# Attention chunks 6 to 11 in halves of 64 tokens on 64x64 tiles, within a fused attention, FFN and expert kernel

## The chip, the cores and the metric

The kernel runs on one core of a Trainium2 chip. The metric is the device time of one execution in microseconds (us); lower is better. Engines are named as the profile names them: PE is TensorE (PEld its weight loads), DVE is VectorE, ACT is ScalarE, POOL is GpSimd, SP is SyncE, which issues most transfers.

## What is computed

Three layers follow each other on 1536 tokens (2 sequences of 768) with a model width of 512. First comes linear attention with decay, 8 heads of width 64, in blocks of 64 tokens:

```python
for b in range(nb):                       # nb = 768 / 64
    qb, kb, vb = (q[:, :, sl], k[:, :, sl], v[:, :, sl])
    intra = einsum('bhic,bhjc->bhij', qb, kb) * Dmask[None]
    intra = einsum('bhij,bhjd->bhid', intra, vb)
    inter = einsum('bhid,bhde->bhie', qb * lam_pow[None], kv_state)
    out[:, :, sl] = intra + inter
    kv_state = lam_block * kv_state + einsum('bhsd,bhse->bhde', kb * rev_pow, vb)
```

`Dmask` holds the powers of each head's decay `lam` below the diagonal. The second layer is a feed-forward block, `elu(x @ w_in) @ w_out`, with an inner width of 2048. The third sends each token that passes a gate to one of 8 experts (inner width 1024) and adds the weighted result. All of it is float32.

## The kernel before

**Chunks.** The kernel takes tokens in 12 chunks of 128, six to a sequence (`CPS`), three to an FFN block of 384 tokens (`CPB`). A chunk holds two of the reference's blocks, which is the same computation with a mask of 128x128 per head and a state that is carried every 128 tokens. Per chunk there are four groups of fp32 matmuls on TensorE. `at_scores` (L246) multiplies keys by queries, 8 matmuls on 64 of the 128 rows of the array each, two heads side by side. `at_pv` (L295) multiplies values by masked scores, 8 matmuls on 64 columns of the array each. `at_inter` (L310) multiplies the state by decayed queries, 4 matmuls on the whole array; the state of two heads stands as a block-diagonal 128x128 matrix. `at_kv` (L338) multiplies decayed keys by values, 8 matmuls on 64 columns each with 64 moving columns. An fp32 matmul shows as two instructions, each with its weight load. Chunks 0 and 6 begin a sequence and lack the product with the state; chunks 5 and 11 end one and have no keys by values.

**Around them.** VectorE applies the mask (`at_mask`, L256) and adds to the state (`at_state`, L363, L365). GpSimd scales queries (`at_qd`, L273), keys (`at_kdec`, L279) and, from chunk 6 on, the old state (`at_decay`, L350). The result leaves PSUM as a rounded part by ScalarE (`at_evac_hi`, L318) and a rest by VectorE (`at_evac_lo`, L324); the FFN multiplies both parts in three passes.

**The FFN.** `ff1_mm` (L390) is 12 matmuls of 384 columns into a bank of tag h, of which there are two. ScalarE takes relu and exp from it (`ff1_act`, L395, L398), VectorE the max (`ff1_max`, L410), ScalarE rounds (`ff1_hi`, L416), and VectorE takes the rest (`ff1_lo`, L421). `ff2` (L437) is three matmuls of 512 columns for one chunk of tokens.

**Order.** From L641 on, every engine runs in the order in which the program is written. The first part follows the list `PLAN`, which holds chunks 0 to 5, the conversion of the FFN weights on ScalarE and VectorE, and the first FFN steps. Then come steps numbered n, from J = 24 on. In a step the program writes: max and rounding of step n + 1, `ff1_mm(n + 2)`, what the lists Y and A hold for n, `ff1_lo(n + 1)`, `ff2(n, 0)`, `ff2(n, 1)`, `ff1_act(n + 2)`, list B, `ff2(n, 2)`, list Z. Chunks 6 to 8 have their scores at steps 24, 26 and 28 (`at_S`, list A) and everything else at 25, 27 and 29 (`at_P`); chunks 9 to 11 have them at 37, 39, 41 and at 38, 40, 42. `at_P` ends with the load of chunk c + 2 on SyncE's queue (L227, L230). The routing of a finished chunk to its expert (`route_T` transposes, `route_pick` takes logits and the largest, `route_rank`, `route_slot` and `route_send` place it) for chunks 0 to 2 starts at steps 25, 26 and 27, one part a step.

**Banks.** PSUM has eight banks: two of tag h, three of tag y and three of tag aux. `aux()` takes from y in steps 24 to 31 and from aux otherwise. A new tile waits until the last reader of the bank that it is given is done.

Of the kernel before, what the change touches and what calls it, by code (L numbers as in the profile page):

```python
# [8 lines left out]
F32 = mybir.dt.float32  # L9
# [7 lines left out]
P = 128  # L17
# [7 lines left out]
NTOK = NBLK * TB  # L25
NCH = NTOK // P
CPS = 6
LEAD = 21
TAIL1 = 8
E = 8  # L30
# [29 lines left out]
def kernel(  # L60
# [35 lines left out]
    def aux():  # L96
        return bank(aux_tag[0], 3)
# [134 lines left out]
    def load_chunk(c, eng=None):  # L232
        alloc_chunk(c)
        dma_kq(c, eng)
        dma_kv(c, eng)
# [46 lines left out]

    o_t = {}

    def at_pv(c, b=None):
        first = c not in o_t
        if first:
            o_t[c] = b if b is not None else aux()
        o = o_t[c]
        v = kv_t[c]  # L290
        for hp in range(4):
            cs = slice(hp * P, (hp + 1) * P)
            for j in range(2):
                h = 2 * hp + j
                nc.tensor.matmul(  # L295
                    out=o[64 * j:64 * j + 64, cs], lhsT=v[:, 1, h * D:(h + 1) * D],
                    rhs=pm_t[c, j][:, hp, :], start=(first and hp == 0),
                    stop=(not first or c % CPS == 0),
                    skip_group_check=True,
                )  # L300
        del pm_t[c, 0], pm_t[c, 1]

    def at_inter(c, b=None):
        if c % CPS:
            qd = qd_t.pop(c)
            first = c not in o_t
            if first:
                o_t[c] = b if b is not None else aux()
            for hp in range(4):
                nc.tensor.matmul(out=o_t[c][:, hp * P:(hp + 1) * P], lhsT=state[:, hp, :],  # L310
                                 rhs=qd[:, hp, :], start=(first and hp == 0), stop=not first,
                                 skip_group_check=True)

    def at_evac_hi(c):
        b, cc = divmod(c, CPB)
        if b not in xT:
            xT[b] = mid.tile([P, 2, 4, TB], F32R, tag="xT", name="xT", bufs=2)
        nc.scalar.activation(out=xT[b][:, 0, :, cc * P:(cc + 1) * P],  # L318
                             in_=o_t[c].rearrange("p (k i) -> p k i", k=4), func=ACTF.Copy)

    def at_evac_lo(c):
        b, cc = divmod(c, CPB)
        ts = slice(cc * P, (cc + 1) * P)
        nc.vector.tensor_tensor(out=xT[b][:, 1, :, ts],  # L324
                                in0=o_t.pop(c).rearrange("p (k i) -> p k i", k=4),
                                in1=xT[b][:, 0, :, ts].bitcast(F32), op=ALU.subtract)

    s_t = {}

    def at_kv(c):  # L330
        if c % CPS == CPS - 1:
# [254 lines left out]
    if True:  # L586
# [127 lines left out]
        for item in PLAN.split():  # L714
            op, args = item.split(":")
            run[op](*map(int, args.split(",")))
            if item == "F1:1":
                tables()
        nc.sync.dma_start(out=wg, in_=wgs.rearrange("(k p) e -> p k e", p=P))
        init_slots()  # L720
        for n in range(LEAD, J):
# [18 lines left out]
        A, B, C, Y, Z = {}, {}, {}, {}, {}  # L740
        early = None

        def at_S(c):
            at_scores(c)
            at_qd(c)
            for half in range(2):
                at_mask(c, half)
            at_kdec(c)

        def at_P(c):  # L750
            at_pv(c)
            at_inter(c)
            at_decay(c)
            at_kv(c)
            at_evac_hi(c)
            at_state(c)
            at_evac_lo(c)
            if c + 2 < NCH:
                load_chunk(c + 2)

        def put(d, n, f, *a):
            d.setdefault(n, []).append((f, a))
# [7 lines left out]
                put(Y, n + 2 + i, route_slot, c0 + i)  # L770
                put(B, n + 2 + i, route_send, c0 + i)

        for i in range(CPB):
            put(A, J + 2 * i + 1, at_P, CPS + i)
            put(A, 2 * NF + 6 + 2 * i, at_P, CPS + CPB + i)
        put_routes(J + 1, 0)
        put_routes(2 * NF, CPB)
        for i in range(CPB):
            put(A, J + 2 * i, at_S, CPS + i)
            put(A, 2 * NF + 5 + 2 * i, at_S, CPS + CPB + i)  # L780
        put_routes(3 * NF, 2 * CPB)
        for n in range(3 * NF, N):
            f = n - 3 * NF
# [324 lines left out]
def layout(inputs):  # L1108
    import numpy as np

    def pair(a):
        a = _chunks(a).reshape(2, 4, 2, CPS, P, D)
        return a.transpose(0, 3, 2, 5, 1, 4).reshape(NCH, P, 4, P)

    def rows(a):
        return _chunks(a)[:, :, :, ::-1].transpose(0, 2, 3, 1, 4).reshape(NCH, P, DM)

    q, k, v = inputs["q"], inputs["k"], inputs["v"]
    def words(a):
        return a.view(np.int64) if a.dtype == np.float64 else a  # L1120

    w_in = words(np.ascontiguousarray(inputs["moe_w_in"])).reshape(4, P, NF, P).transpose(2, 1, 0, 3).reshape(NF, P, DM)
# [12 lines left out]
```

## Time and profile before

| | us |
|---|---|
| median of 3 runs (lowest, highest) | 460.17 (458.51, 460.31) |
| the profiled execution | 458.31 |
| its span, first to last instruction | 456.6 |
| PE busy | 442.7 (97%) |
| DVE busy | 294.1 (64%) |
| ACT busy | 240.3 (53%) |
| POOL busy | 78.4 (17%) |

The profile is of one execution. A busy time is the time in which at least one instruction of the engine is in progress, so matmuls that overlap count once. The granted TensorE clock was 0.997 of full speed over the span.

### The profile page before, as it was taken

How to read it: one execution, taken by the hardware profiler on the slowest of the kernel's cores; microseconds unless marked ns; L12 is line 12 of the kernel's file. 1: busy time of each engine (PE TensorE's matmuls, PEld its weight loads, DVE VectorE, ACT ScalarE, POOL GpSimd, SP SyncE). 2: the span in 40 equal slices, each digit the busy share in tenths (PEclk: the TensorE clock that was granted, in tenths of full speed). 3: DMA queues.
4: the chain of work that ended last, by engine and by line, in shares of the span. 5: the costliest groups of instructions: out<-in, count | busy, mean ns of one | idle time of the engine just before them, and what ended most of it. 6: DMA issues, size and time to landing. Idle time of an engine off the chain costs nothing.

```text
span 456.6 us, 7006 instructions
## 1 busy us (share of the span) xinstructions
PE 442.7 (97%) x2679; PEld 385.9 (85%) x2679; DVE 294.1 (64%) x557; ACT 240.3 (53%) x398; POOL 78.4 (17%) x100
## 2 busy tenths in 40 slices
PE   8899999999999999999999999999999999999993
PEld 7778889878998888998888889889988788888872
DVE  4899999999333455345333324665536688999970
ACT  3465776667344322433222444565653788888840
POOL 4532002200100224104321000130003102222201
PEclk9999999999999999999999999999999999999998
DMA  8999602896001221300020006335248789999401
GB/s 309 407 418 419 246 0 92 248 120 189 0 2 69 94 95 61 134 0 34 16 77 1 0 1 253 105 127 198 93 139 319 260 295 391 363 365 375 175 17 33
DMA packets 26106, 74.65 MB, mean 164 GB/s; under 512 B 4018, under 2 KB 9146, under 8 KB 24016
## 3 DMA queue, kind: packets, MB, share of 16 engines
q1 hardware_dynamic: 24032, 68.99, 42.7%
q0 software_dynamic: 1600, 3.03, 1.8%
q10 hardware_dynamic: 432, 2.10, 1.2%
q8 instruction: 23, 0.38, 0.3%
q14 instruction: 19, 0.16, 0.1%
HBM read 65.82 MB, written 10.51 MB: 167 GB/s over the span
## 4 chain that ended last, share of the span: by engine, by line
PE 76%; DVE 9%; issue 5%; ACT 3%; POOL 2%; DMA 2%; SPq 1%; POOLq 0%; DVEq 0%; ACTq 0%
PE h L390 24%; PE y L437 19%; PE h L918 8%; PE y L943 6%; PE aux L437 5%; DVE v L172 2%; DVE v L175 2%; DMA xe<-blank 2%; PE aux L310 1%; PE aux L295 1%; PE aux L492 1%; PE aux L246 1%; PE aux L929 1%; ACT v L157 1%; PE y L246 1%
## 5 line engine op out<-in xcount | busy, mean ns | idle before, releaser
L390 PE MATMUL h<-xT,wa 128*128 128x384 f32 x480 | 90.1, 338 | 0.0
L390 PEld LDWEIGHTS h<-xT,wa 128*128 128x128 f32 x480 | 83.8, 188 | 3.1 <-DVE e L410 0.4
L437 PE MATMUL y<-wa,g 128*128 128x512 f32 x270 | 70.8, 401 | 0.9 <-DVE g L421 0.9
L395 ACT ACTIVATE e<-h 128x384 f32<-128x384 f32 x64 | 31.1, 486 | 53.2 <-PE h L390 53.1
L437 PEld LDWEIGHTS y<-wa,g 128*128 128x128 f32 x270 | 48.9, 188 | 11.6 <-DVE g L421 1.8
L416 ACT ACTIVATE g<-e 128x384 fp32r<-128x384 f32 x64 | 33.4, 522 | 43.3 <-DVE e L410 43.1
L410 DVE SCALAR_TENSOR_TENSOR e<-e,h 128x384 f32<-128x384 f32 x64 | 35.1, 548 | 31.5 <-ACT e L398 31.5
L390 PE MATMUL h<-xT,wb 128*128 128x384 f32 x288 | 54.3, 338 | 0.0
L390 PEld LDWEIGHTS h<-xT,wb 128*128 128x128 f32 x288 | 50.5, 188 | 1.8
L421 DVE TENSOR_TENSOR g<-e,g 128x384 fp32r<-128x384 f32 x64 | 37.8, 591 | 16.0 <-ACT g L416 15.9
L437 PE MATMUL y<-wb,g 128*128 128x512 f32 x162 | 40.5, 395 | 0.0
L918 PE MATMUL h<-wa,xgT 128*128 128x512 f32 x144 | 36.1, 397 | 0.1
L569 POOL DMA_INDIRECT xe<-x,idx x12 | 12.1, 1009 | 139.7 <-DVE s L542 58.0
L437 PEld LDWEIGHTS y<-wb,g 128*128 128x128 f32 x162 | 30.0, 188 | 5.7 <-DVE g L421 0.2
L398 ACT ACTIVATE e<-e 128x384 f32<-128x384 f32 x64 | 33.6, 525 | 2.0
L918 PEld LDWEIGHTS h<-wa,xgT 128*128 128x128 f32 x144 | 26.5, 188 | 5.7 <-ACT xgT L468 0.3
L135 DVE TENSOR_TENSOR wa<-big,wa 128x1024 fp32r<-128x1024 f32 x22 | 26.6, 1234 | 4.3 <-ACT wa L134 4.1
L943 PE MATMUL y<-wa,ht 128*128 128x512 f32 x96 | 23.7, 398 | 0.0
L135 DVE TENSOR_TENSOR wa<-ahead,wa 128x1024 fp32r<-128x1024 f32 x18 | 21.6, 1246 | 2.9 <-ACT wa L134 2.7
L134 ACT ACTIVATE wa<-big 128x1024 fp32r<-128x1024 f32 x22 | 22.4, 1058 | 1.2 <-DMA big<-in_wex_dram 1.2
L437 PE MATMUL aux<-wa,g 128*128 128x512 f32 x90 | 23.0, 397 | 0.0
L952 POOL TENSOR_TENSOR o<-o,xg 128x512 f32<-128x512 f32 x7 | 9.1, 1294 | 71.5 <-ACT o L951 62.2
(205 smaller groups left out, 682.4 us busy)
## 6 DMA issues: line engine op xcount, KB each, us to landing
big<-in_wex_dram SPq DMA_DIRECT2D x17, 1024.0 KB, 5.0
ahead<-in_wex_dram SPq DMA_DIRECT2D x15, 1024.0 KB, 7.0
wb<-in_wff_dram SPq DMA_DIRECT2D x10, 1024.0 KB, 14.5
big<-in_wff_dram SPq DMA_DIRECT2D x5, 1024.0 KB, 17.5
big<-in_kq_dram SPq DMA_DIRECT2D x6, 512.0 KB, 3.5
big<-in_kv_dram SPq DMA_DIRECT2D x6, 512.0 KB, 4.3
out_dram<-x SPq DMA_DIRECT2D x12, 256.0 KB, 2.2
xg<-xe SPq DMA_DIRECT2D x8, 257.0 KB, 7.2
```

Of the source, the lines that this page charges most:

```text
L134: nc.scalar.activation(out=w[:, 0, cs], in_=src, func=ACTF.Copy)
L135: nc.vector.tensor_tensor(out=w[:, 1, cs], in0=src, in1=w[:, 0, cs].bitcast(F32), op=ALU.subtract)
L390: nc.tensor.matmul(out=h, lhsT=w[:, wi, k * P:(k + 1) * P], rhs=xT[b][:, xi, k, :], start=(j == 0), stop=(j == 11))
L395: nc.scalar.activation(out=e, in_=h_t[n], func=ACTF.Relu, scale=-1.0)
L398: nc.scalar.activation(out=e_t[n], in_=e_t[n], func=ACTF.Exp, scale=-1.0)
L410: nc.vector.scalar_tensor_tensor(out=e, in0=e, scalar=-1.0, in1=h_t.pop(n), op0=ALU.add, op1=ALU.max)
L416: nc.scalar.activation(out=g[:, 0, :], in_=e, func=ACTF.Copy)
L421: nc.vector.tensor_tensor(out=g[:, 1, :], in0=e_t.pop(n), in1=g[:, 0, :].bitcast(F32), op=ALU.subtract)
L437: nc.tensor.matmul(out=y_t[b, t], lhsT=g[:, gi, t * P:(t + 1) * P], rhs=w[:, wi, 512:1024], start=(f == 0 and i == 0), stop=(f == NF - 1 a ...
L569: sc = nc.gpsimd.indirect_dma_start(out=xe[:, :], out_offset=bass.IndirectOffsetOnAxis(ap=idx[:, c:c + 1], axis=0), in_=x2[:, :], in_offse ...
L918: nc.tensor.matmul(out=h, lhsT=xgT_t[e][:, xi, k * P:(k + 1) * P], rhs=w_t[NF + 8 * e + k][:, wi, j * 512:(j + 1) * 512], start=(i == 0), ...
L943: nc.tensor.matmul(out=y, lhsT=ht[:, hi, k, :], rhs=w_t[NF + 8 * e + 4 + k // 2][:, wi, (k % 2) * 512:(k % 2) * 512 + 512], start=(i == 0) ...
```

## The change

In chunks 6 to 11 the halves of 64 tokens are treated as blocks of their own, as the reference has them: the mask is 64x64 per head, the state moves every 64 tokens, and every matmul runs on one of the four 64x64 tiles of the array. All of it that falls in a step is put into one function, `at_X(c, nxt)`: products by values and state of chunk c, then keys by values and scores of the following chunk, then a drain of TensorE and the rest of chunk c's state products. `at_X2` evacuates, loads, and updates the state. There are four such steps for three chunks (24, 26, 28, 29 and 37, 39, 41, 42). The state is a ring of three 64-column tables in `state` and `lp`, updated by four operations on VectorE for each half; queries are scaled into a spare half of `mask`; keys are scaled a step earlier. The excursion's second bank is one of tag h. In chunks 0 to 5 the products stay on 128 tokens, and the state product becomes eight matmuls of 64 columns of the array. The head order in the rows of x changes, and `w_in` is reordered before launch to match. The routing of chunks 0 to 2 moves to steps 25, 27 and 30, with `route_pick` in the step of its `route_T`.

```diff
+    def put_o(c, s, b, kb, lhsT, rhs, n=SB):
+        banks, begun = o_t[c]
+        o = banks[s][SB * b:SB * b + SB, kb * n:(kb + 1) * n]
+        nc.tensor.matmul(out=o, lhsT=lhsT, rhs=rhs, start=(s, b) not in begun, stop=True,
+                         skip_group_check=True)
+        begun.add((s, b))
...
     def at_inter(c, b=None):
         if c % CPS:
             qd = qd_t.pop(c)
-            for hp in range(4):
-                nc.tensor.matmul(out=o_t[c][:, hp * P:(hp + 1) * P], lhsT=state[:, hp, :],
-                                 rhs=qd[:, hp, :], start=(first and hp == 0), stop=not first,
-                                 skip_group_check=True)
+            o_bank(c, b)
+            for kb in range(4):
+                for b in range(2):
+                    hp, a = 2 * (kb // 2) + b, kb % 2
+                    put_o(c, 0, b, kb, state[:, hp, SB * a:SB * a + SB], qd[:, hp, :], P)
...
+    def at_tables():
+        nc.gpsimd.tensor_copy(out=mask[0:SB, :, 0:SB], in_=mask[0:SB, :, SB:P])
+
+    def at_scores2(c, banks):
+        t = kq_t[c]
+        for k in range(4):
+            for a, m in ((0, 0), (1, 1), (0, 1), (1, 0)):
+                r, ts = slice(SB * a, SB * a + SB), slice(SB * m, SB * m + SB)
+                nc.tensor.matmul(out=banks[a][ts, k * SB:(k + 1) * SB], lhsT=t[r, 0, k, ts],
+                                 rhs=t[r, 1, k, SB * (1 - m):SB * (2 - m)],
+                                 start=True, stop=True, skip_group_check=True)
...
+    def at_kv2(c, banks, off=0):
+        t = kv_t[c]
+        for k in range(4):
+            for a, m in ((0, 1), (1, 1)) if last_of(c) else ((0, 1), (1, 0), (1, 1), (0, 0)):
...
+    def at_state2(c, s):
+        if last_of(c) and s:
+            return
+        src, prev = s_t[c][1 - s], state_of(c, s)
+        st_t[2 * c + s + 1] = st = ring3[(2 * c + s) % 3]
+        if prev is None:
+            nc.vector.tensor_copy(out=st, in_=src)
+        else:
+            for k in range(4):
+                nc.vector.scalar_tensor_tensor(out=st[:, k, :], in0=prev[:, k, :],
+                                               scalar=lp[:, k, SB - 1:SB], in1=src[:, k, :],
+                                               op0=ALU.mult, op1=ALU.add)
...
+    def at_out(c, banks):
+        t, pm = kv_t[c], pm_t.pop(c)
+        o_t[c] = banks, set()
+        for kb in range(4):
+            for b, r in ((0, 0), (1, 1), (1, 0), (0, 1)):
+                h, rows = 4 * (kb // 2) + 2 * b + kb % 2, slice(SB * r, SB * r + SB)
+                put_o(c, 1 - r, b, kb, t[rows, 1, h * D:(h + 1) * D], pm[rows, h % 2, h // 2, :])
+        for m in range(2):
+            for b, r in ((0, 0), (1, 1), (1, 0), (0, 1)):
+                inter(c, r, m, 1 - r, b)
+
+    def at_out2(c):
+        nc.tensor.drain()
+        for m in range(2):
+            for b, r in ((0, 0), (1, 1), (1, 0), (0, 1)):
+                inter(c, r, m, r, b)
...
+        def at_X(c, nxt):
+            if c is not None:
+                at_out(c, [aux(), aux()])
+            if nxt is not None:
+                banks = [aux(), bank("h", 2)]
+                at_kv2(nxt, banks, 4 * SB)
+                at_scores2(nxt, banks)
+            if c is not None:
+                at_out2(c)
+            if nxt is not None:
+                for a in range(2):
+                    at_mask2(nxt, a)
+
+        def at_X2(c, nxt):
+            if c is not None:
+                at_evac_hi(c)
+                at_evac_lo(c)
+                if c + 2 < NCH:
+                    load_chunk(c + 2)
+            if nxt is not None:
+                at_state2(nxt, 0)
+                at_qd2(nxt)
...
+        def put_chunks(n, c0):
+            for c, nxt, m in ((None, c0, n), (c0, c0 + 1, n + 2), (c0 + 1, c0 + 2, n + 4),
+                              (c0 + 2, None, n + 5)):
+                put(A, m, at_X, c, nxt)
+                put(B, m, at_X2, c, nxt)
+                if nxt is not None:
+                    if m > J:
+                        put(B, m - 1, at_kdec2, nxt)
+                    put(Z, m, at_state2, nxt, 1)
+
+        at_kdec2(CPS)
+        put_chunks(J, CPS)
+        put_chunks(2 * NF + 5, CPS + CPB)
+        for n, c in zip((J + 1, J + 3, J + 6), range(CPB)):
+            put(B, n, route_T, c)
+            put(Z, n, route_pick, c)
+            put(Z, n, route_exp, c)
+            put(Y, n + 1, route_rank, c)
+            put(Y, n + 1, route_slot, c)
+            put(B, n + 1, route_send, c)
```

## Rows read from the trace of the kernel before

**Rows 1.** The page's busy times: us, share of the span, instructions.
```profile
PE 442.7 (97%) x2679; PEld 385.9 (85%) x2679; DVE 294.1 (64%) x557; ACT 240.3 (53%) x398; POOL 78.4 (17%) x100
```
**Rows 2.** Windows, chunks 9 to 11: length, then each engine's busy us (PE, PEld, DVE, ACT, POOL).
```profile
215.92:252.89 36.97, 36.97 (x280) 31.77 (x278) 13.11 (x25) 10.50 (x21) 9.21 (x12) 1.00 0.10 32
```
**Rows 3.** Chain of waits, chunk 5: start us, us, what.
```profile
33.66 1.93 POOL qd L273
...
37.06 1.13 PE aux L310 x8
...
54.75 1.15 DVE v L172
```
**Rows 4.** TensorE's timeline, steps 37 on: start us, us, engine, line, operation.
```profile
215.92 2.25 PE L390 MATMUL h<-xT,wa 128*128 128x384 f32 x12
218.10 1.16 PE L246 MATMUL aux<-big 64*128 64x128 f32 x16
...
221.40 2.26 PE L390 MATMUL h<-xT,wa 128*128 128x384 f32 x12
223.59 1.09 PE L295 MATMUL aux<-t,big 128*64 128x128 f32 x16
224.61 1.16 PE L310 MATMUL aux<-t,state 128*128 128x128 f32 x8
225.70 0.69 PE L338 MATMUL aux<-big 128*64 128x64 f32 x16
226.32 2.36 PE L437 MATMUL y<-wa,g 128*128 128x512 f32 x9
228.52 2.25 PE L390 MATMUL h<-xT,wa 128*128 128x384 f32 x12
...
252.89 2.25 PE L390 MATMUL h<-xT,wb 128*128 128x384 f32 x12
...
257.06 2.25 PE L390 MATMUL h<-xT,wb 128*128 128x384 f32 x12
```
**Rows 5.** TensorE's timeline, chunks 1 and 2, two groups of one tiling.
```profile
20.75 1.05 PE L295 MATMUL y<-pm_store,wb 128*64 128x128 f32 x16
21.62 1.04 PE L295 MATMUL aux<-pm_store,wb 128*64 128x128 f32 x16
```
**Rows 6.** Windows of 60 ns, L338 alone: length, PE busy, matmuls in flight.
```profile
225.80:225.86 0.06, 0.06 (x4) 1.00 0.00 0
225.86:225.92 0.06, 0.06 (x6) 1.00 0.00 0
```
**Rows 7.** L338 and L246 by source: TensorE's sequencer at their waits.
```profile
L338 PEldq EVENT_SEMAPHORE  x1: 51/51/51, 29.0 to 29.0; - x1
...
L246 PEldq EVENT_SEMAPHORE  x1: 51/51/51, 29.3 to 29.3; - x1
```
**Rows 8.** Timelines of TensorE and VectorE, steps 24 to 27.
```profile
141.47 2.25 PE L390 MATMUL h<-xT,wb 128*128 128x384 f32 x12
...
141.58 0.54 DVE L410 SCALAR_TENSOR_TENSOR e<-e,h 128x384 f32<-128x384 f32 x1
...
156.63 0.22 DVE L506 SCALAR_TENSOR_TENSOR eqd<-y,mx,dact 128x8 f32<-128x8 f32 x1
...
157.44 1.29 DVE L256 TENSOR_TENSOR t<-y,mask 128x512 f32<-128x512 f32 x2
158.64 0.55 DVE L421 TENSOR_TENSOR g<-e,g 128x384 fp32r<-128x384 f32 x1
...
165.21 0.42 DVE L365 TENSOR_TENSOR state<-y,state 64x256 f32<-64x256 f32 x1
```
**Rows 9.** ScalarE's timeline, chunk 7.
```profile
165.04 0.58 ACT L318 ACTIVATE xT<-y 128x512 fp32r<-128x512 f32 x1
```
**Rows 10.** GpSimd's timeline, chunk 7.
```profile
150.31 1.28 POOL L273 TENSOR_TENSOR t<-big,lp 128x512 f32<-128x512 f32 x1 [32.84 <-PE y L295]
```
**Rows 11.** The page's DMA issues: line, count, KB each, median us to landing.
```profile
big<-in_kv_dram SPq DMA_DIRECT2D x6, 512.0 KB, 4.3
```

More of the change, by code (lines that the diff above doesn't have):

```diff
@@ L27 @@
 CPS = 6
+SB = 64
 LEAD = 21
@@ L283, with o_bank @@
     o_t = {}
-    def at_pv(c, b=None):
[L286 to L290, printed above, removed]
-        for hp in range(4):
[L292 to L301, printed above, removed]
+    def put_o(c, s, b, kb, lhsT, rhs, n=SB):
[4 more added lines that the diff above has]
+        begun.add((s, b))
+    def o_bank(c, b=None):
+        if c not in o_t:
+            o_t[c] = [b if b is not None else aux()], set()
+    def at_pv(c, b=None):
+        o_bank(c, b)
+        for kb in range(4):
+            for b in range(2):
+                h = 4 * (kb // 2) + 2 * b + kb % 2
+                put_o(c, 0, b, kb, kv_t[c][:, 1, h * D:(h + 1) * D], pm_t[c, h % 2][:, h // 2, :], P)
     def at_inter(c, b=None):
@@ L305, in at_inter @@
             qd = qd_t.pop(c)
[L306 to L309, printed above, removed]
-                nc.tensor.matmul(out=o_t[c][:, hp * P:(hp + 1) * P], lhsT=state[:, hp, :],
-                                 rhs=qd[:, hp, :], start=(first and hp == 0), stop=not first,
-                                 skip_group_check=True)
+            o_bank(c, b)
+            for kb in range(4):
+                for b in range(2):
+                    hp, a = 2 * (kb // 2) + b, kb % 2
+                    put_o(c, 0, b, kb, state[:, hp, SB * a:SB * a + SB], qd[:, hp, :], P)
@@ new lines @@
+    pairs = mask.rearrange("p (k a) i -> p a k i", a=2)
+    spare = mask.rearrange("p (k s) i -> p k s i", s=2)[:, :, :, SB:P]
+    ring3 = [state[:, :, 0:SB], state[:, :, SB:P], lp[:, :, SB:P]]
+    def at_tables():
[8 more added lines that the diff above has]
+                                 start=True, stop=True, skip_group_check=True)
+        sc_t[c] = banks
@@ new lines, in at_mask2, with at_qd2 @@
+    def at_mask2(c, a):
+        if c not in pm_t:
+            pm_t[c] = t2().rearrange("p k i -> p (k i)").rearrange("p (a k i) -> p a k i", a=2, k=4)
+        nc.vector.tensor_tensor(
+            out=pm_t[c][:, a], in0=sc_t[c][a][:, 0:4 * SB].rearrange("p (k i) -> p k i", k=4),
+            in1=pairs[:, a, :, 0:SB], op=ALU.mult)
+    def at_qd2(c):
+        for s in range(2):
+            if c % CPS or s:
+                nc.gpsimd.tensor_tensor(out=spare[:, :, s], in0=kq_t[c][:, 1, :, SB * s:SB * s + SB],
+                                        in1=lp[:, :, 0:SB], op=ALU.mult)
@@ new lines, in at_kdec2, with last_of @@
+    def at_kdec2(c):
+        k3 = kv_t[c][:, 0, :].rearrange("p (h d) -> p h d", h=H)
+        nc.gpsimd.tensor_tensor(out=k3, in0=k3, in1=mask[:, :, SB - 1:SB].to_broadcast([P, H, D]),
+                                op=ALU.mult)
+    s_t, st_t = {}, {}
+    def last_of(c):
+        return c % CPS == CPS - 1
+    def at_kv2(c, banks, off=0):
+        t = kv_t[c]
+        for k in range(4):
+            for a, m in ((0, 1), (1, 1)) if last_of(c) else ((0, 1), (1, 0), (1, 1), (0, 0)):
+                r = slice(SB * m, SB * m + SB)
+                h = 2 * k + a
+                nc.tensor.matmul(out=banks[m][SB * a:SB * a + SB, off + k * SB:off + (k + 1) * SB],
+                                 lhsT=t[r, 0, h * D:(h + 1) * D], rhs=t[r, 1, h * D:(h + 1) * D],
+                                 start=True, stop=True, skip_group_check=True)
+        s_t[c] = [b[:, off:off + 4 * SB].rearrange("p (k e) -> p k e", k=4) for b in banks]
@@ new lines, in state_of @@
+    def state_of(c, s):
+        return None if c % CPS == 0 and s == 0 else st_t[2 * c + s]
+    def at_state2(c, s):
[10 more added lines that the diff above has]
+                                               op0=ALU.mult, op1=ALU.add)
@@ new lines, in inter @@
+    def inter(c, r, m, s, b):
+        st = state_of(c, s)
+        rows, k = slice(SB * r, SB * r + SB), b + 2 * m
+        if st is None:
+            lhsT, rhs = zrow[rows, 0:SB], kq_t[c][rows, 1, k, SB * s:SB * s + SB]
+        else:
+            lhsT, rhs = st[rows, k, :], spare[rows, k, s, :]
+        put_o(c, s, b, 2 * m + r, lhsT, rhs)
+    def at_out(c, banks):
+        t, pm = kv_t[c], pm_t.pop(c)
+        o_t[c] = banks, set()
+        for kb in range(4):
+            for b, r in ((0, 0), (1, 1), (1, 0), (0, 1)):
[4 more added lines that the diff above has]
+                inter(c, r, m, 1 - r, b)
@@ L314, in at_evac_hi, with halves @@
+    def at_out2(c):
[3 more added lines that the diff above has]
+                inter(c, r, m, r, b)
+    def halves(c):
+        b, cc = divmod(c, CPB)
+        banks = o_t[c][0]
+        n = P // len(banks)
+        for s, bank_s in enumerate(banks):
+            ts = slice(cc * P + n * s, cc * P + n * s + n)
+            yield bank_s[:, 0:4 * n].rearrange("p (k i) -> p k i", k=4), xT[b], ts
     def at_evac_hi(c):
-        b, cc = divmod(c, CPB)
+        b = c // CPB
@@ L316, in at_evac_hi @@
         if b not in xT:
             xT[b] = mid.tile([P, 2, 4, TB], F32R, tag="xT", name="xT", bufs=2)
-        nc.scalar.activation(out=xT[b][:, 0, :, cc * P:(cc + 1) * P],
-                             in_=o_t[c].rearrange("p (k i) -> p k i", k=4), func=ACTF.Copy)
+        for o, x, ts in halves(c):
+            nc.scalar.activation(out=x[:, 0, :, ts], in_=o, func=ACTF.Copy)
     def at_evac_lo(c):
[L322 to L326, printed above, removed]
@@ L328 @@
-    s_t = {}
+        for o, x, ts in halves(c):
+            nc.vector.tensor_tensor(out=x[:, 1, :, ts], in0=o, in1=x[:, 0, :, ts].bitcast(F32),
+                                    op=ALU.subtract)
+        del o_t[c]
     def at_kv(c):
@@ L718 @@
                 tables()
+        at_tables()
         nc.sync.dma_start(out=wg, in_=wgs.rearrange("(k p) e -> p k e", p=P))
@@ L741 @@
         early = None
[L743 to L759, printed above, removed]
+        def at_X(c, nxt):
[19 more added lines that the diff above has]
+                at_qd2(nxt)
         def put(d, n, f, *a):
@@ L1120, in words @@
         return a.view(np.int64) if a.dtype == np.float64 else a
-    w_in = words(np.ascontiguousarray(inputs["moe_w_in"])).reshape(4, P, NF, P).transpose(2, 1, 0, 3).reshape(NF, P, DM)
+    w_in = words(np.ascontiguousarray(inputs["moe_w_in"])).reshape(2, 2, 2, D, NF, P)
+    w_in = w_in.transpose(4, 1, 3, 0, 2, 5).reshape(NF, P, DM)
     w_out = words(np.ascontiguousarray(inputs["moe_w_out"])).reshape(NF, P, DM)
```

7 lines of the change are left out of this document (removed).

## The prediction

> **What bounds the kernel now.** I read the page's busy table first: TensorE is busy 97% of the span, every other engine 64% or less [rows 1]. A share over 457 us says nothing of one stage, so next came the windows. In the stretch that the change rewrites last (chunks 9 to 11) TensorE is busy for all of 36.97 us, VectorE for 13 and ScalarE for 10 [rows 2]. Whatever TensorE time goes there comes off the end, and whatever makes TensorE wait there is added. The third view was TensorE's timeline: a step without attention repeats after 257.06 - 252.89 = 4.17 us, a step with scores takes 221.40 - 215.92 = 5.48, and one with the products by v and state takes 228.52 - 221.40 = 7.12 [rows 4]. So a chunk's scores cost 1.31 us and the rest of it 2.95. For chunks 0 to 5 I followed the chain of waits, which there passes through GpSimd's qd and back to TensorE [rows 3] and by 55 us has gone over to the weight conversions on VectorE [rows 3].
>
> **What goes.** The second block costs 36.97 - 6 x 4.17 = 11.95 us [rows 2, 4]. In the first, chunk 6 lacks the product with the state; its second part is the 2.95 less the product's 225.70 - 224.61 = 1.09 and some 0.15 of switching, about 1.7. Block one is 3 x 1.31 + 2 x 2.95 + 1.7 = 11.5. Together 23.5 us.
>
> **What comes: products.** An fp32 matmul is two instructions in the trace (8 calls, x16). A chunk needs 16 matmuls for scores, 16 for keys by values (8 in chunk 11, on two tiles, the same time), 16 for scores by values and 16 for the state: 128 instructions, 384 in a block. Their speed is the first unknown, since the trace has no 64x64 tile. It has each direction alone. Row halves (L246, x16) and the full array (L310, x8) both take 1.09 us to the next group [rows 4], so two row halves run beside each other; column halves likewise, 16 in 21.62 - 20.75 = 0.87 [rows 5]. With 64 columns (L338) two more are in flight after every further 60 ns, on a tile of half the width [rows 6]: a tile takes 60 ns per instruction. If four tiles run abreast, an instruction costs 15 ns. If only two do, it costs 30. I take 15: row pairs share their output partitions in two banks, column pairs their input partitions, and both pair up now without loss; four tiles combine the two. Four abreast ask for eight instructions (loads included) in 60 ns. TensorE's sequencer can do that: it stood at a wait ahead of L338 at 29.0 us and was at the one ahead of the following L246 at 29.3, past 32 instructions [rows 7], so about 9 ns each by rounded times. A block: 384 x 0.015 = 5.76 us.
>
> **Excursions.** Scores alone cost 1.31 us against 0.87 of work for 16 half tiles, so entering and leaving another tiling costs 0.44. A block now has four excursions (before, six groups, most of the second kind with the full array between two column tilings): 4 x 0.44 = 1.76. The drain before the last state products is new. A matmul of 64 columns is followed by its tile's next after 60 ns but three pairs are in flight [rows 6], so to empty the array costs two or three such intervals, about 0.16 us, and the first instructions after any wait come late by some 0.1. I take 0.3, three a block: 0.9; bounds 0.1 (the switch alone) and 1.1 (as much as the whole state product L310). A block costs 5.76 + 1.76 + 0.9 = 8.4 us, both 16.8. **Saved: 23.5 - 16.8 = 6.7 us.**
>
> **The wait that is added: a bank of h.** Scores and keys-by-values of the next chunk now take one of the two banks of tag h. ff1_mm of the next step needs a bank again. In the plain step ff1_mm starts at 141.47, before the max that frees the other bank (141.58, 0.54 us) [rows 8]: it gets the bank that was freed earlier. By the same order the next one gets the excursion's, whose last reader is at_state2(nxt, 0), ahead of Z. TensorE has nine ff2 matmuls before it wants it: 228.52 - 226.32 = 2.20 us. VectorE in that time, from the start of ff2 as zero: two masks of half size begin at -0.45, since the drain and the state products stand between scores and ff2. Two of full size took 1.29 and 256 columns took 0.42 [rows 8], so 0.36 apart: free at 0.26. Then ff1_lo (L421, the next starts 0.47 later) to 0.73; two halves of evac_lo, 0.36 apart, to 1.45, with evac_hi on ScalarE (0.58 for a full one [rows 9]) ahead of them from 0.1; four state updates of 64 columns, each between 0.13 and 0.28 (L506, 8 columns, 0.22, is nearest), say 0.19: the last ends at 2.3. With the semaphore 2.4: **0.2 us late**, in the four excursions that carry two chunks; after an excursion without evacuation it is done near 2.0 and nothing waits. Cost 4 x 0.2 = 0.8, bounds 0 and 4 x 0.6. Behind the waiting ff1_mm the whole of TensorE's queue stands, so it is paid in full; relu and exp of that ff1_mm then come as much later, a step ahead of need.
>
> **Routing.** route_pick of chunks 0 to 2 moves into the step of its route_T, behind ff2(n, 2). Copying x2T takes as long as a full evacuation, 0.58 to 0.69, from the end of the transposes, and three ff2 instructions cover about 0.75 with what is in flight: 0 to 0.3 late, I take 0.15, three times: 0.45. VectorE's small operations go with it; its next max is then due only a step later.
>
> **What hides.** kdec and qd on GpSimd (512 columns each, 1.28 for qd [rows 10]) keep their size; kdec moves to the step before, qd behind the excursion, and each has over 4 us until it is read (chunk 8 and 11: 2.2 + 2.1 us of ff2 and ff1_mm). load_chunk(c + 2) goes past evac_lo into B: keys and values land 4.3 us after issue [rows 11], kdec makes it 5.6, and the next excursion but one is 8.5 us away; without that cover each would cost its 1 us. The table copy is one GpSimd operation in idle time (100 operations in all [rows 1]); the halves of evac_hi add about 0.15 us to a ScalarE that is idle for 70% there. Reordering w_in is done before launch.
>
> **Chunks 0 to 5.** A state product of four full matmuls (x8) becomes eight on two column halves (x16): by the pair rows above both are 0.87. Only mode changes go, five of them (two each around chunks 3 and 4, one at 5), 0.1 to 0.15 each. The chain passes two: the one before L310 of chunk 4, on which qd (33.66) waits, and the one after L310 of chunk 5 (37.06) [rows 3]. I take 0.2 saved; bounds 0 (VectorE takes over by 55 us) and 0.7.
>
> **Sum.** -6.7 + 0.8 + 0.45 - 0.2 = -5.65 us. The profiled execution took 458.31 (span 456.6, the rest around it), which gives 452.7. It lies below all three timed runs (458.51 to 460.31, median 460.17); from the median it is 454.5. I forecast **454.0**.
>
> **Rivals.** *The tiles leave two abreast.* At 30 ns, the fastest mean in rows 6, a block's products are 11.5 us, with 2.66 of overhead 14.2, both 28.3: 4.8 slower than 23.5; with 0.45 and -0.2 the time is 460.2 + 5.05 = 465.2 (the bank is then free early, since masks run beside the longer products with the state). For it: no row has four tiles; against it: each pairing is free now. It decides from 22 ns per instruction: 768 x 0.022 + 5.3 + 1.05 = 23.2, and there the change saves nothing at all and the time stays at 460. *The h bank waits longer.* If ff1_mm gets the other bank, it waits for the max of its predecessor, behind four more state updates (0.76) and the max itself (0.55): 1.5 late four times, 0.85 twice, 7.7 in place of 0.8, and 461.4, no change. Against it is the plain step [rows 8]. *The drain costs a microsecond* (upper bound): six times 0.8 more than taken, 459.3.
>
> The Trainium skill speaks for the first rival: "TensorE: Matmul & The Clock Gate", section "Wait — 56ns, not 53.3ns?", states a floor of about 25 ns from start to start of matmuls, however few the columns, and "TensorEngine Tiling (Array Packing)", section "Instruction Overhead", advises against tiling a dimension that is already small. No run here shows a mean below that floor, so the trace does not refute it. By it the two blocks would be 768 x 0.025 + 5.3 = 24.5 us, an estimate, and the time near 461.
>
> **Chances.** Forecast 0.68 (own range 451 to 457.5), two abreast 0.15, bank wait 0.10, drain 0.07. A measurement here tells 0.5% (2.3 us) from no change. Faster: the forecast's 0.68 and a little of the drain's, 0.69; same: 0.16, the rest of the bank's and the drain's; slower: the first rival's 0.15. The range 450.5 to 461.5 leaves out that 0.15 above and some 0.04 at the ends.
>
> **What would show it.** Four abreast: an excursion that carries two chunks lasts 2.7 us between ff1_mm and ff2, eight or more in flight where L338 now has its pairs. Right on the bank: gaps of TensorE before L390 in the step after, released by VectorE's state update, 0 to 0.4 us each; wrong: released by L410's max and over 1 us. Drain: a hole of 0.3 us within the excursion. The forecast fails if those excursions take over 3.6 us, which is where the two blocks stop saving.

## The result and the profile after

The changed kernel takes **453.88 us**, median of 8 runs (453.55 to 456.75); the kernel before, timed beside it, 460.16 (458.48 to 460.44, 8 runs). The ratio is **0.9884, 95% interval [0.9862, 0.9907]**. The forecast was 454.0. The two profiled executions lie closer together than the medians: 458.31 before and 454.56 after, a difference of 3.75 where the medians differ by 6.28. Executions of one program differ by TensorE's clock in the last routing stage (shown below), so the steps of the prediction are held against the traces, up to where that stage begins.

The busy times of the changed kernel answer to [rows 1]:
```profile
PE 437.1 (97%) x3159; PEld 379.6 (84%) x3159; DVE 297.4 (66%) x594; ACT 242.4 (54%) x404; POOL 79.5 (18%) x100
```
TensorE has 480 more matmuls and is busy for 5.6 us less. The share is still 97%: it stays the bound.

TensorE's timeline of the changed kernel answers to [rows 4]: step 39, whose excursion carries two chunks, and the start of the two steps behind it (start us, us, engine, line, operation, then in brackets the idle time before it and what ended it). L495 is ff1_mm, L291 the products by values and state, L363 keys by values, L329 the scores, L542 ff2.
```profile
224.70 2.25 PE L495 MATMUL h<-xT,wa 128*128 128x384 f32 x12
...
227.62 0.22 PE L363 MATMUL aux<-big 64*64 64x64 f32 x1
227.63 0.22 PE L363 MATMUL h<-big 64*64 64x64 f32 x1
227.64 0.22 PE L363 MATMUL aux<-big 64*64 64x64 f32 x1
227.65 0.22 PE L363 MATMUL h<-big 64*64 64x64 f32 x1
227.68 0.22 PE L363 MATMUL aux<-big 64*64 64x64 f32 x1
...
228.52 0.22 PE L329 MATMUL h<-big 64*64 64x64 f32 x1
228.90 0.26 PE L291 MATMUL aux<-mask,lp 64*64 64x64 f32 x1 [0.16 <-issue]
...
229.29 0.50 PE L542 MATMUL y<-wa,g 128*128 128x512 f32 x1
...
231.59 0.42 PE L495 MATMUL h<-xT,wb 128*128 128x384 f32 x1
...
235.85 0.34 PE L495 MATMUL h<-xT,wb 128*128 128x384 f32 x1
```
Four tiles start within 0.03 us, and the first of them takes its next matmul at 227.68, some 0.06 after 227.62. The drain shows as the step from 228.52 to 228.90. The step lasts 231.59 - 224.70 = 6.89; a plain one lasts 4.17 [rows 4].

Windows of 60 ns of the same excursion (length, PE busy, matmuls in flight, clock) answer to [rows 6], where 4 and 6 stood:
```profile
226.97:227.03 0.06, 0.06 (x8) 1.00 0.00 0
227.03:227.09 0.06, 0.06 (x12) 1.00 0.00 0
...
228.20:228.26 0.06, 0.06 (x18) 1.00 0.00 0
```
Four more are in flight after each further window, twice as many as with column halves.

The starts of ff1_mm on TensorE's timelines, us, and the length of two stretches (last step included), for all kernels of this study (edits below; "tail" is from step 61 to the end of the span):

| kernel | step 24 | steps 24 to 31 | steps 37 to 43 | step 61 | tail |
|---|---|---|---|---|---|
| before | 141.47 | 49.13 | 41.14 | 332.46 | 124.1 |
| after | 142.46 | 47.08 | 37.91 | 328.21 | 124.4 |
| e1, after again | 142.92 | 47.08 | 37.90 | 328.66 | 127.3 |
| e2 | 141.48 | 47.07 | 37.90 | 327.20 | 125.8 |
| e3 | 141.88 | 48.41 | 40.41 | 331.43 | 124.3 |
| e4 | 141.93 | 48.80 | 39.30 | 330.77 | 124.2 |
| e5 | 142.78 | 47.08 | 37.91 | 328.52 | 125.7 |
| e6 | 139.90 | 46.72 | 37.56 | 324.94 | 124.2 |
| e7, one run | 142.82 | 48.11 | 38.91 | 330.60 | 125.7 |
| e8, before again | 141.70 | 49.13 | 41.14 | 332.69 | 124.3 |
| e9 | 139.70 | 49.13 | 41.14 | 330.69 | 125.7 |
| e10 | 141.95 | 46.72 | 37.56 | 326.97 | 124.1 |

From before to after the first block gives 2.05 us and the second 3.23. **The first 24 steps lose 1.0**, and 0.3 is lost in the tail.

### The profile page after: what moved, and what is told of

It reads as the page before. It is cut to its first block, busy times and chain, and to the rows that moved or that the text cites. A ratio compares the mean times of both kernels' runs of the same rounds, so it can differ in the third digit from the quotient of the medians.

```text
span 452.6 us, 8014 instructions
## 1 busy us (share of the span) xinstructions
PE 437.1 (97%) x3159; PEld 379.6 (84%) x3159; DVE 297.4 (66%) x594; ACT 242.4 (54%) x404; POOL 79.5 (18%) x100
## 4 chain that ended last, share of the span: by engine, by line
PE 69%; DVE 16%; issue 7%; ACT 5%; POOL 1%; DMA 1%; POOLq 0%; DVEq 0%; ACTq 0%
PE h L495 21%; PE y L542 17%; PE h L1042 8%; PE y L1067 6%; PE aux L542 5%; DVE v L175 4%; DVE v L178 3%; ACT v L160 2%; DVE wa L189 2%; DVE g L526 2%; DVE v L172 1%; PE aux L291 1%; PE aux L597 1%; PE y L291 1%; PE aux L1053 1%
## 5 line engine op out<-in xcount | busy, mean ns | idle before, releaser
L495 PE MATMUL h<-xT,wa 128*128 128x384 f32 x480 | 90.4, 339 | 0.3 <-DVE e L515 0.3
L495 PEld LDWEIGHTS h<-xT,wa 128*128 128x128 f32 x480 | 83.6, 188 | 3.8 <-DVE e L515 1.0
L542 PE MATMUL y<-wa,g 128*128 128x512 f32 x270 | 70.7, 401 | 1.1 <-DVE g L526 0.9
L542 PEld LDWEIGHTS y<-wa,g 128*128 128x128 f32 x270 | 49.0, 188 | 11.7 <-DVE g L526 1.8
L495 PE MATMUL h<-xT,wb 128*128 128x384 f32 x288 | 54.5, 338 | 0.0
L495 PEld LDWEIGHTS h<-xT,wb 128*128 128x128 f32 x288 | 50.3, 188 | 2.9 <-issue 1.3
L526 DVE TENSOR_TENSOR g<-e,g 128x384 fp32r<-128x384 f32 x64 | 39.2, 613 | 19.3 <-ACT g L521 19.1
L542 PE MATMUL y<-wb,g 128*128 128x512 f32 x162 | 40.8, 396 | 0.2 <-DVE g L526 0.2
L542 PEld LDWEIGHTS y<-wb,g 128*128 128x128 f32 x162 | 29.9, 188 | 6.4 <-DVE g L526 0.8
L542 PE MATMUL aux<-wa,g 128*128 128x512 f32 x90 | 22.8, 396 | 0.0
```

Of the source, the lines that this page charges most:

```text
L495: nc.tensor.matmul(out=h, lhsT=w[:, wi, k * P:(k + 1) * P], rhs=xT[b][:, xi, k, :], start=(j == 0), stop=(j == 11))
L526: nc.vector.tensor_tensor(out=g[:, 1, :], in0=e_t.pop(n), in1=g[:, 0, :].bitcast(F32), op=ALU.subtract)
L542: nc.tensor.matmul(out=y_t[b, t], lhsT=g[:, gi, t * P:(t + 1) * P], rhs=w[:, wi, 512:1024], start=(f == 0 and i == 0), stop=(f == NF - 1 a ...
```

## The experiments

**The same programs again (e1, e8).** No edit.

> The changed kernel itself, for its spread. If the microsecond that the first 24 steps lost in the profile (ff1_mm of step 24 starts at 142.46 against 141.47 before) comes from GpSimd's two moved operations standing beside VectorE's conversions, this profile shows it again: the weight operations beside them last 1.6 and 2.1 us in place of 1.22, and step 24 starts near 142.4. If it is jitter of transfers, step 24 starts anywhere from 141 to 143 and the two long operations are gone or elsewhere. Ratio to before 0.987 to 0.991.

> The kernel before, unchanged, for a second profile. The timed runs of before lie in two groups, near 458.5 and 460.2. If the groups come from the granted clock in the last routing stage (0.50 there in one profile of the changed kernel, which then took 3.2 us longer), a run near 460 shows a stretch at half clock between 341 and 349 us and the same steps up to there; if they come from the conversions, steps 9 to 23 differ from the first profile. A run near 458.5 should repeat the first profile within 0.3 us at every step.

e1 took 454.9 (453.77 to 458.55, 9 runs; ratio 0.9914 [0.9887, 0.9941] to 459.06 before). Its blocks repeat to 0.01 us, and step 24 comes 142.92 - 141.70 = 1.22 later than in e8: the loss in the first 24 steps is in both pairs. One half of the expectation was missed: the conversion beside the table copy takes 1.63 again, but kdec of chunk 6 starts only at 111.98 here, and the operation that it stretches is another one (L526 at 112.60, 1.42 in place of 0.56), while the conversion that took 2.08 takes 1.22. Step 16 is 0.50 longer than in before all the same. In e4, where kdec starts at 110.34, step 16 is only 0.06 longer, so what kdec costs hangs on where it falls. e8 (one run, 458.74) repeats the steps of before within 0.23. e1's profiled execution took 457.95, 3.4 more than the changed kernel's first, of which 2.9 lie behind step 61. Windows over its last routing stage (length, busy us of PE, PEld, DVE, ACT and POOL, granted clock, DMA share, GB/s):
```profile
329.00:341.00 12.00, 12.00 (x77) 10.74 (x75) 5.16 (x15) 5.51 (x10) 0.00 (x0) 0.99 0.44 159
341.00:345.00 4.00, 4.00 (x22) 3.88 (x23) 1.56 (x8) 0.00 (x0) 0.00 (x0) 0.50 1.03 418
345.00:349.00 4.00, 3.91 (x24) 3.63 (x23) 2.37 (x17) 1.18 (x4) 0.82 (x1) 0.68 0.86 317
```
and the same stretch of the changed kernel's first profile:
```profile
341.00:345.00 4.00, 3.91 (x38) 3.70 (x37) 2.98 (x22) 1.11 (x4) 0.00 (x0) 1.00 1.03 416
```
From 341 to 345 us the granted clock is 0.50 (1.2 GHz of the two levels), and for a part of the next window as well, behind a stretch in which TensorE was busy throughout; 22 matmuls are in progress in place of 38. The same program, an execution apart, so this is not the change.

**The two GpSimd operations put behind the first evacuation (e2, e5).**
```diff
-        at_tables()          # right after the PLAN loop
...
-        at_kdec2(CPS)        # ahead of put_chunks
...
+        at_tables()          # behind the evacuation of frame 0
+        at_kdec2(CPS)
```
In e2 the two stand in the other order, so the keys of chunk 6 are scaled by tables that are not yet copied; e5 has the right order. Of e2 only the times are used.

> The changed kernel with the mask table's copy and the first keys' scaling on GpSimd issued only after the first evacuation, past the conversions of the FFN weights. Theory of the shared port: both weight operations are back at 1.22 us, step 24 starts 0.9 to 1.4 us earlier than in the unmoved kernel, near 141.2, and the time is 0.9 to 1.4 us lower. Rival, jitter of transfers: no operation on VectorE gets shorter for it and the time is the same within 0.3 us. Second rival: the time is lost later instead, because keys' scaling then ends after step 24 wants it; the excursion at step 24 would start late by up to 1 us.

> The changed kernel with the mask table's copy and then the first keys' scaling on GpSimd issued after the first evacuation. Theory of the shared port, with what the run before showed: step 24 starts at 141.5 (142.46 to 142.92 in two profiles of the unmoved kernel), no weight operation on VectorE over 1.3 us between 88 and 112 us but for the one beside GpSimd's own conversion, and the end 1.0 us earlier. The two operations take 2.0 us from about 117, and the excursion of step 24 is 27 us later, so nothing waits. Rival, that a profile's first 24 steps scatter by that much of themselves: step 24 anywhere between 141.5 and 143.

e2 took 454.91 (453.15 to 457.96, 7 runs; ratio 0.9907 [0.9875, 0.9939]), e5 454.55 (453.72 to 456.34, 6 runs; ratio 0.9887 [0.986, 0.9915]). The total doesn't tell them from the changed kernel, the steps do: step 12 lasts 5.07 in e2 and 5.04 in e5 (5.50 after, 5.07 before), step 16 lasts 4.17 in both (4.67 after, 4.17 before). In e2 step 24 starts at 141.48, the time of before. e5's step -1 was 1.3 late (39.97 against 38.65 in after): its granted clock was 0.50 from 30.6 to 34.0 us, which hides its gain in step 24. From step -1 to step 24 e5 takes 102.81 and e2 102.85, where after takes 103.81 and e1 103.76. GpSimd's timeline of e5 shows both operations beside a gap of VectorE, which idles from 117.49 to 119.03:
```profile
117.72 0.60 POOL L322 COPY mask<-mask 64x512 f32<-64x512 f32 x1
118.40 1.07 POOL L349 TENSOR_TENSOR big<-big,mask 128x512 f32<-128x512 f32 x1
```

**State parts on column halves alone (e3):** the changed kernel with at_S and at_P of before in chunks 6 to 11 and no tables; it keeps the eight 64-column matmuls of the state product, in all chunks, and the new head order.

> One part alone: the new head order and the state product as eight column-half matmuls in all chunks; chunks 6 to 11 stay on 128 tokens with the old two groups of steps. Theory: a product with the state on column halves costs the same 0.87 us and saves only the changes of tiling to its neighbours, so steps 27, 29, 38, 40 and 42 are each 0.1 to 0.25 shorter than before (8.59, 7.20, 7.12, 7.12, 6.31), 0.9 us in all; of the 0.2 to 0.6 saved in chunks 0 to 5 nothing is left at step 24, since VectorE's conversions set the pace by then. Time 0.5 to 1.2 us under before. Rival: column halves do not pair in the state product, then each of those steps is 0.9 longer.

e3 took 457.97 (456.78 to 459.62, 12 runs; ratio 0.9974 [0.9958, 0.999]). Steps 27, 29, 38 and 40 are 0.36 shorter each, more than was expected, and step 42 by only 0.02, less than was expected. Over both blocks that is 1.4 us, without any 64x64 tile. TensorE's timeline of e3, step 38, beside [rows 4]:
```profile
223.28 1.09 PE L291 MATMUL aux<-t,big 128*64 128x128 f32 x16
224.20 1.04 PE L291 MATMUL aux<-t,state 128*64 128x128 f32 x16
225.08 0.64 PE L443 MATMUL aux<-big 128*64 128x64 f32 x16
225.64 2.37 PE L542 MATMUL y<-wa,g 128*128 128x512 f32 x9
```
From 223.28 to ff2 it is 2.36 in place of 226.32 - 223.59 = 2.73: the group that used the full array between two column tilings costs 0.36 in changes of tiling, a third of the 1.09 that it seemed to take. In chunks 0 to 5 the same saving does not show: step 24 comes at 141.88, no earlier than in before. This execution had a granted clock of 0.50 from 31.0 to 34.4 us, so it tells little by itself; but e2, without that, has step -1 0.5 ahead of before (38.63 against 39.14) and step 24 at the same time as before.

**Two tiles at a time (e4):** the order of matmuls in scores and keys by values.
```diff
-        for k in range(4):
-            for a, m in ((0, 0), (1, 1), (0, 1), (1, 0)):
+        for am in (((0, 0), (1, 1)), ((0, 1), (1, 0))):
+            for k, a, m in [(k, a, m) for k in range(4) for a, m in am]:
```

> The changed kernel with scores and keys-by-values ordered so that only two of the four tiles are in use at a time (same matmuls, same results). Theory (a tile takes 58 ns per instruction and four run abreast): the 32 instructions of each group take 0.94 in place of 0.47 us, so the excursion at step 24 is 0.9 us longer and the whole time 11 x 0.47 = 5.2 us longer, near 459. Rival (the rate is set by issue, 15 ns per instruction whatever the tile): no change within 0.5 us.

e4 took 457.62 (457.0 to 461.54, 12 runs; ratio 0.9979 [0.9958, 0.9999]). From step 24 to step 61 it is 3.1 us longer than after, where 5.2 was expected. TensorE's timeline of e4:
```profile
218.42 0.22 PE L363 MATMUL h<-big 64*64 64x64 f32 x1
218.43 0.22 PE L363 MATMUL aux<-big 64*64 64x64 f32 x1
218.48 0.22 PE L363 MATMUL h<-big 64*64 64x64 f32 x1
218.49 0.22 PE L363 MATMUL aux<-big 64*64 64x64 f32 x1
```
Two start per 60 ns, so an instruction costs 30 ns while one pair is at work; at the seams between groups the tiles of the next pair already start beside the old ones, which gives part of it back. A tile's own next matmul comes 58 to 60 ns on, whether one or three others are at work.

**A second drain (e7, one run of 458.36):** `nc.tensor.drain()` between at_kv2 and at_scores2.

> The changed kernel with a second drain of TensorE, between keys-by-values and scores of the next chunk, six in all. Theory: a drain costs what the hole in the trace shows (0.38 us from the last start before it to the first after it, less one interval of 0.06), so steps 24, 26, 28, 37, 39 and 41 are 0.3 longer each. Rival 1: a drain costs only the pipeline's emptying, 0.16. Rival 2: part of the hole is a wait for operands of the state product, then the second drain costs under 0.1.

The six excursions that have both products grow by 0.31 to 0.35 each (step 39: 7.24 for 6.89). TensorE's timeline of e7 around the added drain:
```profile
218.94 0.22 PE L363 MATMUL aux<-big 64*64 64x64 f32 x1
219.27 0.26 PE L329 MATMUL aux<-big 64*64 64x64 f32 x1
```
A drain costs 0.33, as the prediction's 0.3 had it. A kernel without any drain wasn't run.

**All of GpSimd's work off the conversions (e6), and its parts (e9, e10).** e6 is e5 with `ON_POOL = ()`, by which VectorE does the conversion steps of frames 7 and 10, and with at_state2(nxt, 0) ahead of the evacuation in at_X2. e9 is the kernel before with `ON_POOL = ()` alone, e10 is e6 without it.
```diff
-    ON_POOL = (7, 10)
+    ON_POOL = ()
...
         def at_X2(c, nxt):
+            if nxt is not None:
+                at_state2(nxt, 0)
             if c is not None:
                 at_evac_hi(c)
...
-                at_state2(nxt, 0)
```

> As the run above, and two edits more: the first state update of the next chunk goes ahead of the evacuation on VectorE, and the two weight rests that GpSimd computes (frames 7 and 10) go to VectorE. Theory of the shared port: GpSimd's 3.1 and 2.4 us stretch a VectorE operation by 2.1 and 1.9, while on VectorE each costs 1.14, so the conversions end 0.8 + 0.8 us earlier and step 24 starts near 139.9. State first: ff1_mm after an excursion with two chunks is no longer 0.09 late, steps 26, 28, 39, 41 shorter by 0.09 each, 0.35 in all. Together 2 us under the run above. Rival for the weights: VectorE is in order, so the extra 1.14 us stands ahead of what TensorE waits for and step 24 does not move or starts up to 1 us later.

> The kernel before with one change: the conversion steps of frames 7 and 10 that GpSimd did (3.13 and 2.41 us there) are done by VectorE (1.22 us each). Theory: what they cost is VectorE's time, since VectorE's operation beside each stretches by about 2 us (3.30 and 2.46 in place of 1.22 and 0.55), so the gain of e6 in its first 24 steps belongs to this edit and not to the attention: steps 9, 13 and 14 shrink by 0.1, 0.9 and 0.7, step 24 starts at 139.9 to 140.1 (141.47 and 141.70 before) and the rest keeps its length: 1.5 us faster, a median of 458.6. Rival: part of e6's gain is the 0.5 us by which the 64-token tiles bring TensorE ahead in chunks 0 to 5, which VectorE no longer swallows once it is faster: then step 24 comes at 140.4 to 140.5 here, 1.0 us faster, 459.1. Second rival: on VectorE the two operations only add to its chain, and step 24 stays at 141.5 or later.

> e5 with at_state2(nxt, 0) ahead of the evacuation and GpSimd's two conversion steps left where they were. It tells apart the two parts of e6. Theory: ff1_mm waits about 0.1 us for the state update's bank after the excursions that carry two chunks, so steps 26 to 29 and 39 to 42 shrink by some 0.08 to 0.1 each where an excursion went before, 0.4 to 0.5 us in all; step 24 stays at 141.5 and the time is 454.1 to 454.2 where e5 took 454.55. Rival: evac_lo is now 0.38 later and the transposed activations that ff1_mm reads with it, so the wait only changes its releaser and nothing is won (454.5).

**e6 takes 450.56 (450.15 to 450.98, 5 runs; ratio 0.9798 [0.9772, 0.9824] to the kernel before) and beats both kernels.** e9 takes 458.06 (456.43 to 458.31, 6 runs; ratio 0.9948 [0.993, 0.9965]), e10 453.86 (453.01 to 454.35, 4 runs; ratio 0.9873 [0.9857, 0.9889]). In e9 step 24 starts at 139.70, 1.8 ahead of before and even ahead of e6: the whole early gain of e6 belongs to this edit, and what the state product on column halves saves in chunks 0 to 5 does not show at step 24 with a faster VectorE either. Steps 12 and 13 are 0.9 shorter each in e9 than in before (the expectation counts them 13 and 14). In e10 steps 26 to 29 and 39 to 42 shrink by 0.06 to 0.10 each, from step 24 to step 44 by 0.70 against e5. VectorE's timeline of e10, against the one of after in the next section, has the state update ahead of evac_lo:
```profile
228.57 0.55 DVE L526 TENSOR_TENSOR g<-e,g 128x384 fp32r<-128x384 f32 x1
229.03 0.85 DVE L381 SCALAR_TENSOR_TENSOR lp<-state,lp,h 128x64 f32<-128x64 f32 x4
229.80 0.75 DVE L430 TENSOR_TENSOR xT<-aux,xT 128x256 fp32r<-128x256 f32 x2
```
e9's profile also has the clock of e1. Its windows over the last routing stage:
```profile
342.00:343.00 1.00, 1.00 (x13) 1.00 (x12) 0.69 (x5) 0.01 (x1) 0.00 (x0) 1.00 1.00 397
343.00:344.00 1.00, 1.00 (x8) 1.00 (x8) 0.93 (x6) 0.00 (x0) 0.00 (x0) 0.69 1.04 426
344.00:345.00 1.00, 1.00 (x9) 0.94 (x8) 0.50 (x3) 0.00 (x0) 0.00 (x0) 0.50 1.00 406
```
Its tail is 125.7, and it took 458.11. That is 1.6 to 1.7 longer than its two shortest runs (456.43 and 456.50) and 1.6 longer in the tail than before's profile (124.1), in a program that differs from before only in the first 90 us.

## Why the prediction came out as it did

**Products: right.** 15 ns per instruction were taken; 16 starts in 0.233 us are 14.6. What speaks for four abreast over faster issue is e4: with only pairs ready the excursions grow. The Trainium skill's floor of about 25 ns from start to start ("TensorE: Matmul & The Clock Gate", section "Wait — 56ns, not 53.3ns?") does not hold between different tiles: here they start 7 ns apart, and only a tile's own next matmul waits for 58 ns. The prediction looked at means, of which 30 ns was the lowest, and held that the trace did not refute the floor. It did: the two column halves of L338 start at 225.866 and 225.873 in before, also 7 ns apart. The rival that rested on 30 ns is refuted; the Trainium skill's "TensorEngine Tiling (Array Packing)", section "Instruction Overhead", which the prediction weighed beside it, did not decide here.

**Excursion and drain: right.** 2.66 was the working for an excursion with two chunks (128 x 0.015 + 0.44 + 0.3); step 39 is 6.89 - 4.17 - 0.09 of wait = 2.63. The first of a block, with scores and keys by values alone, is 5.55 - 4.17 = 1.38 (1.40 by the terms). The hole at the drain, 0.38 less one interval, is 0.32.

**Bank of h: right in place, and the size nearly.** VectorE's timeline of the changed kernel behind step 39's excursion (ff2 starts at 229.29):
```profile
228.79 0.42 DVE L337 TENSOR_TENSOR t<-aux,mask 128x256 f32<-128x256 f32 x1 [4.34 <-PE h L329]
229.13 0.42 DVE L337 TENSOR_TENSOR t<-h,mask 128x256 f32<-128x256 f32 x1
229.46 0.55 DVE L526 TENSOR_TENSOR g<-e,g 128x384 fp32r<-128x384 f32 x1
229.93 0.75 DVE L430 TENSOR_TENSOR xT<-aux,xT 128x256 fp32r<-128x256 f32 x2
230.59 0.85 DVE L381 SCALAR_TENSOR_TENSOR lp<-state,lp,h 128x64 f32<-128x64 f32 x4
```
The masks start at -0.50 (predicted -0.45), are 0.34 apart (0.36), and the last state update ends at 231.44 - 229.29 = 2.15 (2.3). ff1_mm follows at 231.59, about 0.1 late and not 0.2. The wait is too short for the view of waits to name a releaser; that it hangs on the state updates is shown by e10, where their move alone takes 0.10 off the step. It takes as much off the plain step behind, which the prediction did not have: eight times 0.09 = 0.7 in place of four times 0.2. That the total fits is luck: half the wait, paid twice as often. The rival that the bank waits for the max, 1.5 us, is refuted with it, as e7 refutes a drain of a microsecond.

**Routing: nearly right.** Between the last three ff2 instructions and route_pick's first matmul lie 152.71 - 151.78 = 0.93 us at step 25, 1.03 at step 27 and 0.93 at step 30, on TensorE's timeline of the changed kernel; in before the same three ff2 instructions take 153.27 - 152.49 = 0.78 to the next ff1_mm. That is 0.55 late in all, for 0.45.

**The two blocks together: right.** The terms gave 23.5 - 16.8 - 0.8 - 0.45 = 5.45 us; measured are 2.05 + 3.23 = 5.28.

**The step that failed: "The table copy is one GpSimd operation in idle time", with kdec and chunks 0 to 5.** GpSimd is idle there, but VectorE is not, and by then VectorE sets the pace. Predicted were 0.2 saved in the first 24 steps; measured are 1.0 and 1.2 lost, a term wrong by 1.2 to 1.4 us, and the largest error of the sum. GpSimd's timeline of the changed kernel:
```profile
87.01 2.40 POOL L189 TENSOR_TENSOR wb<-v,wb 128x1024 fp32r<-128x1024 f32 x1 [13.72 <-ACT wb L183]
89.35 0.94 POOL L322 COPY mask<-mask 64x512 f32<-64x512 f32 x1
109.35 1.06 POOL L349 TENSOR_TENSOR big<-big,mask 128x512 f32<-128x512 f32 x1 [19.05 <-DMA big<-in_kv_dram]
```
VectorE's timeline of the changed kernel beside these three:
```profile
87.38 2.45 DVE L526 TENSOR_TENSOR g<-e,g 128x384 fp32r<-128x384 f32 x1 [0.47 <-ACT g L521]
89.75 1.63 DVE L175 SCALAR_TENSOR_TENSOR v<-wb,v 128x1024 int32<-128x1024 int32 x1
...
109.41 2.08 DVE L189 TENSOR_TENSOR wb<-v,wb 128x1024 fp32r<-128x1024 f32 x1
```
and of the kernel before, the operations that answer to them:
```profile
87.30 2.46 DVE L421 TENSOR_TENSOR g<-e,g 128x384 fp32r<-128x384 f32 x1 [0.47 <-ACT g L416]
89.68 1.21 DVE L172 SCALAR_TENSOR_TENSOR v<-wb,v 128x1024 int32<-128x1024 int32 x1
...
108.93 1.23 DVE L186 TENSOR_TENSOR wb<-v,wb 128x1024 fp32r<-128x1024 f32 x1
```
The conversion beside the table copy takes 1.63 for 1.21, the one beside kdec of chunk 6 takes 2.08 for 1.23. In before that kdec stood at 116.43, where VectorE idled. TensorE waits for VectorE in this stretch, by its waits from 66 to 120 us in the changed kernel (what waited, releaser: us in all, times, longest):
```profile
PE y L542 <- DVE g L526: 1.1, 3, 0.6
PE h L495 <- DVE e L515: 0.3, 1, 0.3
```
and, less, in before:
```profile
PE y L437 <- DVE g L421: 0.9, 2, 0.6
```
So 0.43 and 0.50 of the delays reach the path in steps 12 and 16, and the 0.5 by which TensorE is ahead at step -1 is used up by step 9, where ff1_mm waits for VectorE's max and starts at 77.00 against 76.94 in before. e2 and e5 take the two delays away by moving the two operations, nothing else. Before's own trace had the warning: its L421 at 87.30 took 2.46, where another takes 0.55 [rows 8], beside a GpSimd operation that ran from 86.94 for 2.41. Taking that one and its twin away is the 1.8 us of e9 and nearly all of what e6 gains on e10 (326.97 - 324.94 = 2.03 at step 61).

**Why 454.0 was met all the same.** The traces saved 332.46 - 328.21 = 4.25 at step 61 where 5.65 was worked out. The forecast was then set against a base of 454.0 + 5.65 = 459.65, between the profiled execution and the median of 460.17, which lies 1.9 above it, without a reason for these 1.9. e9 gives one: with the same tail program, an execution with a clock of 0.50 in the last routing stage is 1.6 longer. That before's median is of such executions, and the changed kernel's 453.88 mostly not, fits most of the gap (4.25 and 1.6 against 6.28). Of the 49 runs of before that were timed beside the experiments, the 19 with a mean granted clock of 0.985 or 0.992 took 459.88 to 460.63, and the two with 0.997 took 458.61 and 458.65; but 0.991 stands beside 458.20 and 460.43 alike, and two of the changed kernel's shortest runs (453.55, 453.78) had 0.988. A run's mean does not say where its clock fell, and no profile caught before itself with the fall, so this stays likely and not shown. Between the shortest runs of both the difference is 458.48 - 453.55 = 4.93. The forecast met the time by luck: 1.4 too much saved by the sum, and a difference of medians that is 2.0 larger than what the traces save.

## What to carry to other kernels

An engine's idle time is a hiding place only if the operation leaves its neighbours alone: before putting work on GpSimd, look at what VectorE does in that window and whether VectorE is what the bound engine waits for, and look in the trace for an operation that takes far longer beside GpSimd than elsewhere. Small matmuls on disjoint quarters of the array are priced per tile, with four tiles sharing one interval, if their order in the program interleaves all four. When a profiled execution and the median differ by more than the effect, work out the sum against the profile and find out where the difference lies before carrying it over.

## What the runs showed of the hardware

- **GpSimd holds VectorE up.** GpSimd's operation ends at 87.01 + 2.40 = 89.41, and VectorE's, begun at 87.38 and 0.55 long elsewhere, at 89.83; kdec ends at 110.41, and the conversion beside it at 111.49, 1.08 later (1.23 is its own length). VectorE thus hardly advances until GpSimd is done. It goes the other way too: in e1 kdec starts at 111.98, in the middle of a conversion on VectorE that takes its usual 1.22, and kdec itself takes 1.62 in place of 1.06. The Trainium skill says as much ("SBUF — State Buffer", section "Who interferes with whom"): a VectorE instruction with two inputs in SBUF contends with a GpSimd instruction that reads SBUF, and the one that comes second is blocked in full. The trace agrees; each of these has two inputs there. With GpSimd's part gone (e6) the same operation takes its usual time, on VectorE's timeline of e6:
```profile
86.49 1.23 DVE L189 TENSOR_TENSOR wb<-v,wb 128x1024 fp32r<-128x1024 f32 x1
87.64 0.55 DVE L526 TENSOR_TENSOR g<-e,g 128x384 fp32r<-128x384 f32 x1
```
- **64x64 tiles start 7 ns apart**, four in 58 ns; a drain between such groups costs 0.32 to 0.35 us, and a group on the full array between two column tilings 0.36 in changes.
- **TensorE's granted clock falls to 0.50 in the last routing stage in some executions** of a program and not in others (e1, e2, e5, e7 and e9, but not before, after, e3, e4, e6, e8 and e10). The tail is then 1.3 to 2.9 us longer than in a profile of the same tail program without it. In e3 and e5 the clock also was 0.50 for 3.4 us from about 31 us on. What decides it was not found.
